# Reordering the first 285 entries of a hand-listed schedule in a fused Mamba-2 and SiLU-MLP kernel

## The chip, the cores and the metric

The kernel runs on one core of a Trainium2 chip. A core has five engines that run side by side and meet only through semaphores: TensorE (PE in the profile; its weight loads are shown as PEld), VectorE (DVE), ScalarE (ACT), GpSimd (POOL) and SyncE (SP), which here only issues DMAs. The metric is the device time of one launch in microseconds (us), a median over several runs.

## The reference, cut to what matters

The first half is a chunked state-space scan over 4 batches, 8 heads, 768 steps, head size 32 and state size 16. The second half sends its output, as 3,072 rows of 256, through an MLP.

```python
for c in range(nc):                       # chunks of the sequence
    cum = np.cumsum(log_a[chunk])
    M = (C @ B.T) * exp(cum_i - cum_j) * causal
    y = M @ x + (C @ state) * exp(cum)
    state = exp(sum(log_a)) * state + (B * exp(cum_end - cum)).T @ x
h = y @ w_in                              # 256 -> 2048
out = (h * sigmoid(h)) @ w_out            # 2048 -> 256
```

The two weight matrices come as 64-bit floats. The kernel loads them as pairs of 32-bit words and puts each 32-bit weight together from bits of both words.

## The kernel before, in words

The sequence is cut into 12 units of 256 steps, three to a batch, and two units form a pair. For each unit the scan part makes a decay mask, the product of C and B under that mask, the chunk states and the output y. The MLP then runs pair by pair. `w_in` and `w_out` are cut into 8 blocks each; the blocks of `w_in` are numbered 0 to 7, those of `w_out` 8 to 15.

Nothing is placed automatically. One string, `SCHEDULE`, lists 1,309 entries, and the last loop of the function walks it and calls a function for each. An entry is a name and its numbers: `w,4,2` calls `w_bits(4, 2)`. An entry sends its instructions to one fixed engine, or to the queue that issues its DMA, so the list sets the order in which each engine works; an engine never passes an instruction that waits. Across engines only data and buffers count. The entries that matter here, with their lines in the profile:

- `z` (L441): one 128x512 bf16 matmul on zeros, which does no work for the result and fills TensorE before there is work.
- `ia`, `ir`, `ip` (L375, L383, L379): loads of the decays `a` on SP. `A`, `AT`, `AU` (L448, L453, L457) clip them, transpose them on TensorE, and copy them out.
- `as`, `ab`, `E` (L495 on DVE or L497 on ACT, L502, L512): spread the decays, transpose them, and scan them on DVE to unit u's mask. `P01` (L475, L479): the prefix products, on DVE, from what `ip` loaded.
- `Ln`, `Lt`, `Lx` (L254, L262, L269): loads of B and C in two layouts and of x. An `Ln` moves 64 KB in 1,024 pieces, an `Lx` 128 KB in 1,024 pieces, an `Lt` 32 KB. The last number is the issuing queue: 0 is SP, 1 is ACT.
- `T` (L525), `tp`, `tq` (L531, L540), `ce` (L546): put C and B the other way round and scale them. `g0` (L585) multiplies them on TensorE into the banks `ga` and `gb`; `M` (L600) multiplies the result by the mask, on DVE.
- `B` (L520, POOL), `D` (L571), `S` (L613, L615, DVE), `SM` (L623, ACT): decayed B, its product with x, the running states, and the scaled states. `Y` (L635 with the states, L644 with the mask products) writes the unit's output over `ga` and `gb`; `X0` (L666, ACT) copies it out.
- `lw` (L288): the load of one weight block, 512 KB, on SP. `u`, `v` (L294, L297, ACT) turn its high and low words into floats. `w,n,0` and `w,n,1` (L303, L307, DVE) clip and shift the first; `w,n,2` (L310, DVE) puts the sign of the high word into the second. `W` (L318, POOL) adds both to the finished block. `H`, `lD`, `dD` (L322, L326, L330) split a block into parts.
- `s`, `si` (L697, L703): the first MLP product for one unit and one block, and SiLU. `n1` (L761): the second product of pair 0. `xh`, `x` (L679; L651 or L654): the split of y. `a`, `ax`, `d`, `dg` (L800, L811, L800, L821): the first product of later pairs in parts. `q` (L782): their second product.
- `AA`, `AD` (POOL), `AP` (DVE), `La`, `Lp` (SP): the decays of the later units, by way of DRAM.

`SLOTS` lists, for each of four buffer pools, which buffer each new tile takes, in the order of the list. A tile in a buffer that was used before waits until the last reader of the old tile is done.

Two lines show how an entry becomes an instruction and where the order comes from:

```python
            nc.vector.scalar_tensor_tensor(out=v, in0=hi, scalar=0x80000000, in1=v,
                                           op0=ALU.bitwise_and, op1=ALU.bitwise_or)
...
            f, *q = tok.split(",")
            DO[f](*map(int, q))
```

Of the kernel before, what the change touches and what calls it, by code (L numbers as in the profile page):

```python
# [15 lines left out]


SCHEDULE = """
Ln,0,0,0,1 ia,1 ci z,1 z,1 z,1 z,1 z,1 z,1 ia,0 Ln,0,0,1,1 cI z,1 ch cP ct ip,0,0 z,1 z,1 z,1 c1 cd A AT cp AU lw,0 z,1
z,1 as,0,0 ab,0,0 P01,0,0 P01,0,1 as,0,1 ab,0,1 as,1,1 ab,1,1 E,0,0 u,0 z,1 z,1 z,1 Lt,0,1,3,0 v,0 w,0,0 w,0,2 w,0,1  # L20
lw,4 W,0,1 z,1 B,0,0 z,1 z,1 v,4 Lt,0,1,1,0 u,4 z,1 z,1 Ln,1,1,1,0 z,1 E,0,1 B,0,1 z,1 z,1 z,1 Lt,0,1,0,0 Lt,0,1,2,0
T,0,1 as,1,0 z,1 z,1 z,1 tp,0 tq,0 E,1,1 Lx,0,0,0 Lx,0,1,0 D,0 S,0,0 z,1 w,4,2 z,1 S,0,1 z,1 w,4,0 S,0,2 ce,0,0 ce,0,1
g0,0 M,0,1 lw,7 v,7 Ln,1,0,0,0 SM,0,0 M,0,0 z,1 z,1 SM,0,1 u,7 w,4,1 w,7,0 z,1 z,1 w,7,2 w,7,1 lw,5 v,5 w,5,2 W,0,0
S,0,3 Ln,1,1,0,0 ab,1,0 E,1,0 C,0 Y,0 X0,0,1 Ln,1,0,1,0 B,1,1 X0,0,0 u,5 w,5,0 ip,1,0 z,1 P01,1,0 tp,1 tq,1 s,0,0 ce,1,1
ce,1,0 g0,1 Lx,1,1,0 Lx,1,0,0 W,4 xh,0 w,5,1 si,0,0 B,1,0 P01,1,1 D,1 s,0,4 M,1,1 lw,1 u,1 lw,12 S,1,0 W,5 v,1 ca S,1,1
S,1,2 SM,1,0 SM,1,1 lw,13 s,0,5 si,0,5 v,12 C,1 M,1,0 Y,1 w,1,0 w,1,1 W,7 si,0,4 lw,8 w,1,2 W,1,0 z,1 w,12,2 X0,1,0 H,7
S,1,3 X0,1,1 x,0,0 lD,7 u,12 w,12,0 w,12,1 u,13 w,13,0 w,13,1 W,1,1 s,0,1 u,8 v,8 s,1,5 ir,3 w,8,0 si,0,1 s,1,0 co
Ln,2,0,1,0 xh,1 W,12 x,1,0 w,8,1 v,13 w,13,2 W,13 lw,15 u,15 w,8,2 Ln,2,1,1,0 si,1,5 s,1,4 a,0,7 si,1,4 n1,9,0 H,12
Wd,12 x,0,1 lw,14 u,14 n1,11,0 n1,9,1 x,1,1 W,8 Ln,2,1,0,0 v,14 w,14,2 ir,0 si,1,0 n1,1,0 n1,1,1 H,0 n1,0,1 H,1 lw,6 v,6
w,6,2 n1,11,1 n1,10,1 ir,2 ir,1 u,6 lw,10 Wl,12 AA,0 AA,1 AD,4 w,6,0 AP w,6,1 AD,0 lw,2 Ln,2,0,0,0 ax,0,7 w,15,0 u,10  # L30
u,2 W,6 n1,8,0 AD,1 v,2 H,6 v,10 w,2,0 s,1,1 si,1,1 lw,3 tp,2 dD,7 v,3 v,15 u,3 w,2,1 w,2,2 W,2,0 Lt,3,1,3,0 lD,6 dD,6
w,14,0 n1,8,1 w,3,2 a,0,6 ax,0,6 w,15,2 W,2,1 s,1,2 si,1,2 H,2 d,0,7 w,14,1 dg,0,7 AD,2 w,3,0 w,15,1 d,0,6 dg,0,6 W,14
Lt,3,1,0,0 w,10,2 s,0,2 lw,9 u,9 v,9 Lt,3,1,2,0 Lt,3,1,1,0 T,3,1 H,4 si,0,2 n1,10,0 Lx,2,0,0 n1,12,1 La,2,0,0 w,3,1 tq,2
La,2,1,0 E,2,1 E,2,0 lD,4 w,9,0 W,15 n1,15,1 Lt,3,0,0,0 n1,12,0 B,2 ce,2,0 ce,2,1 Lt,3,0,3,0 g0,2 lw,11 u,11 Lp,2,0 C,2
M,2,1 Lx,2,1,0 gd,2 b,2,0 b,2,1 S,2,0 S,2,1 H,15 S,2,2 W,3 Lp,3,0 Lt,4,1,1,0 H,13 La,3,1,0 w,10,0 v,11 Lt,4,1,0,0
# [853 lines left out]
```

## Time and profile before

| what | value |
|---|---|
| three runs | 328.6, 329.49, 329.88 us; median 329.49 us |
| the profiled execution | 329.1 us, of which 327.4 us are the span of the instructions |
| granted TensorE clock, mean | 0.999 |
| busy share: PE, PEld, DVE, ACT, POOL | 98%, 74%, 73%, 64%, 17% |
| DMA | 29.27 MB in 94,962 packets |

The busy share is an average over stages. The first 18 us of the span hold loads, constants and unit 0's scan; the MLP's first useful matmul (L697) starts at 17.94 us. From there TensorE works without a break up to the last few microseconds. A row of the timeline gives the start, the length, the engine, the line and the tiles of some instructions in a row; in brackets stands how long the engine sat idle ahead of it and what ended that.

### The profile page before, as it was taken

To read this page: it belongs to the slowest core of one execution; us is meant where nothing else is said; L and a number is where in the kernel's file an instruction comes from. 1 tells how busy PE (TensorE), PEld (TensorE's weight loads), DVE (VectorE), ACT (ScalarE), POOL (GpSimd) and SP (SyncE) were. 2 spreads that over 40 slices of the span, in tenths; PEclk is the share of its full clock that TensorE was granted. 3 is DMA by queue.
4 is the path that set the end of the run, shared out by engine and by line. 5 is a ranking of instruction groups with operands and counts; after the bars stand their busy time and mean duration, and the time that the engine had idled before them with its cause. 6 is when DMAs were issued, how large, how long until landed. Compare 5 with 4: busy or idle time off the path is not lost.

```text
span 327.4 us, 7519 instructions
## 1 busy us (share of the span) xinstructions
PE 320.3 (98%) x3064; PEld 243.4 (74%) x3067; DVE 240.4 (73%) x331; ACT 209.5 (64%) x319; POOL 56.0 (17%) x74
## 2 busy tenths in 40 slices
...
GB/s 162 206 200 272 296 175 192 51 148 135 148 127 46 105 115 53 86 36 64 147 74 70 44 1 117 104 26 96 3 74 37 7 2 2 0 88 0 2 1 64
DMA packets 94962, 29.27 MB, mean 89 GB/s; under 512 B 80000, under 2 KB 86912, under 8 KB 94928
## 3 DMA queue, kind: packets, MB, share of 16 engines
...
## 4 chain that ended last, share of the span: by engine, by line
PE 94%; SPq 2%; DMA 1%; DVE 1%; issue 1%; DVEq 0%
PE hp L782 29%; PE ga L800 18%; PE gb L800 18%; PE hp L761 9%; PE hp L697 6%; PE o_ps L782 6%; PE ga L635 2%; PE ga L585 2%; PE ga L644 2%; DMA s2k<-in_C_dram 1%; PE gb L644 1%; PE ga L571 1%; SPq L262 0%; SPq L375 0%; PE o_ps L531 0%
## 5 line engine op out<-in xcount | busy, mean ns | idle before, releaser
L782 PE MATMUL hp<-r4k,s2k 128*128 128x512 f32 x400 | 110.0, 394 | 0.0
L651 DVE SCALAR_TENSOR_TENSOR r4k<-r4k,r4k 128x1024 fp32r<-128x1024 f32 (+1 forms) x42 | 50.5, 1202 | 51.3 <-ACT r4k L827 48.2
L782 PEld LDWEIGHTS hp<-r4k,s2k 128*128 128x128 f32 x400 | 74.0, 188 | 16.4 <-issue 0.3
L800 PE MATMUL ga<-raw,s2k 128*128 128x512 f32 x240 | 62.3, 395 | 0.0
L800 PE MATMUL gb<-raw,s2k 128*128 128x512 f32 x240 | 61.1, 390 | 0.0
L800 PEld LDWEIGHTS ga<-raw,s2k 128*128 128x128 f32 x240 | 44.7, 188 | 11.4 <-ACT ga L811 0.9
L800 PEld LDWEIGHTS gb<-raw,s2k 128*128 128x128 f32 x240 | 44.8, 188 | 9.9 <-ACT gb L811 0.5
L837 DVE SCALAR_TENSOR_TENSOR r4k<-r4k,r4k 128x1024 fp32r<-128x1024 f32 x40 | 49.2, 1231 | 3.4 <-DVE r4k L651 0.9
L827 ACT ACTIVATE r4k<-r4k 128x1024 fp32r<-128x1024 f32 x40 | 42.2, 1058 | 3.2 <-issue 1.3
L811 ACT ACTIVATE ga<-ga 128x1024 f32<-128x1024 f32 x21 | 21.1, 1007 | 24.6 <-PE ga L800 23.8
L811 ACT ACTIVATE gb<-gb 128x1024 f32<-128x1024 f32 x21 | 21.2, 1009 | 17.6 <-PE gb L800 13.3
L782 PE MATMUL o_ps<-r4k,s2k 128*128 128x512 f32 x80 | 30.7, 390 | 0.0
L761 PE MATMUL hp<-r4k,s2k 128*128 128x512 f32 x64 | 30.0, 602 | 0.0
L821 ACT ACTIVATE r4k<-gb 128x1024 f32<-128x1024 f32 x21 | 21.4, 1021 | 12.4 <-PE gb L800 9.9
L520 POOL TENSOR_TENSOR BT<-bn,ab 128x256 f32<-128x256 f32 x10 | 6.7, 672 | 129.5 <-DVE ab L512 123.3
L318 POOL TENSOR_TENSOR s2k<-s2k,s2k 128x512 uint32<-128x512 uint32 (+1 forms) x19 | 23.6, 1250 | 26.4 <-DVE s2k L307 13.7
L821 ACT ACTIVATE r4k<-ga 128x1024 f32<-128x1024 f32 x21 | 21.5, 1023 | 8.4 <-PE ga L800 8.2
L512 DVE TENSOR_TENSOR_SCAN ab<-ab,diag 128x512 f32<-128x512 f32 x20 | 24.8, 1265 | 0.0
L697 PE MATMUL hp<-r4k,s2k 128*128 128x256 f32 x96 | 22.3, 382 | 0.2 <-issue 0.2
L697 PEld LDWEIGHTS hp<-r4k,s2k 128*128 128x128 f32 x96 | 18.0, 190 | 4.0 <-issue 1.4
L761 PEld LDWEIGHTS hp<-r4k,s2k 128*128 128x128 f32 x64 | 11.6, 189 | 10.5 <-issue 9.6
L782 PEld LDWEIGHTS o_ps<-r4k,s2k 128*128 128x128 f32 x80 | 15.0, 188 | 3.2
...
## 6 DMA issues: line engine op xcount, KB each, us to landing
...
```

What stands on the lines that cost most here:

```text
L318: nc.gpsimd.tensor_tensor(out=u[:, :, fs], in0=u[:, :, fs], in1=v[:, :, fs], op=ALU.add)
L512: nc.vector.tensor_tensor_scan(out=o, data0=src, data1=diag.rearrange("p h t -> p (h t)"), initial=0.0, op0=ALU.mult, op1=ALU.add)
L644: nc.tensor.matmul(out=y[w][32 * q:32 * q + 32, c, 64 * k:64 * k + 64], lhsT=xc[64 * c:64 * c + 64, k, h], rhs=m[64 * c:64 * c + 64, k, h] ...
L651: nc.vector.scalar_tensor_tensor(out=l, in0=f32(h), scalar=BACK, in1=y, op0=ALU.mult, op1=ALU.add)
L697: nc.tensor.matmul(out=hp[:, i], lhsT=WT[j][:, kc, 128 * i:128 * i + 128], rhs=XM()[:, 2 * kc:2 * kc + 2, u], start=(kc == 0), stop=(kc == ...
L761: nc.tensor.matmul(out=NP[m], lhsT=WT[8 + f // 2][:, f % 2, 128 * m:128 * m + 128], rhs=GT[0, f // 2][:, f % 2], start=(n == 1), stop=(n = ...
L782: nc.tensor.matmul(out=ACC[P, c], lhsT=WK[8 + i, p][:, k, 128 * m:128 * m + 128], rhs={"h": HT, "l": LT, "d": DT}[p][P, i][:, k], start=(n ...
L800: nc.tensor.matmul(out=o, lhsT=WK[j, q][:, kc, 128 * i:128 * i + 128], rhs=xs[:, 2 * kc:2 * kc + 2], start=(start and q == "h" and kc == 0 ...
L811: nc.scalar.activation(t, t, AF.Copy, scale=1.0 + Z)
L821: nc.scalar.activation(g, t, AF.Silu, scale=BACK)
L827: nc.scalar.activation(t, GT[G, i], AF.Copy, scale=-LESS * Z)
L837: nc.vector.scalar_tensor_tensor(out=DT[G, i], in0=f32(HT[G, i]), scalar=-1.0, in1=f32(LT[G, i]), op0=ALU.mult, op1=ALU.subtract)
```

## The change

The first 285 entries of `SCHEDULE` stand in another order; the entries themselves are the same, and from there on the list is as it was. `SLOTS` is written anew to fit. From about entry 460 on every tile follows the same earlier tile in its buffer as before, only the buffer's number differs. In the order of each engine:

- DVE: `T,0,1` comes before `w,0,1`; `w,4,2`, which stood between `S,0,0` and `S,0,1`, now stands behind `M,0,0` and `M,0,1`. `E,1,0` comes before `w,7,0`, and `w,5,2` is now the last of block 5's three steps. `x,0,1` and `x,1,1` come later, `x,1,1` behind `w,15,2`.
- ACT: `tq,0` and `ce,0,1` come ahead of `u,4` and `v,4`, `ce,0,0` behind them. `SM,0,1` stands before `u,7`, `SM,0,0` between `u,7` and `v,7`.
- TensorE: fourteen `z` stand before `AT` where there were ten; one `z` that stood behind `Y,1` has moved ahead of `s,0,0`. Seven `z` now stand between `ab,0,0` and `tp,0`, with `ab,0,1` and `ab,1,1` behind `tp,0`. In the pair-0 part some `n1` and `s` change places.
- SP: `ir,3` is now second in the queue, and `ir,1`, `ir,0`, `ir,2` are earlier. `lw,4` moves from sixth to twelfth, behind the four `Lt,0` and behind both `Ln,1,1`. The order of later blocks is 12, 8, 13, 2, 6, 14, 10, 15, 3 where it was 12, 13, 8, 15, 14, 6, 10, 2, 3.
- POOL: `ca` and `co`, three memsets, come first; `W,4` comes before `B,1,1`; `W,1` before `W,7`; `AA,1` and `AA,0` come around `W,13`. The two `Ln` on ACT's queue change places.

```diff
-Ln,0,0,0,1 ia,1 ci z,1 z,1 z,1 z,1 z,1 z,1 ia,0 Ln,0,0,1,1 cI z,1 ch cP ct ip,0,0 z,1 z,1 z,1 c1 cd A AT cp AU lw,0 z,1
-z,1 as,0,0 ab,0,0 P01,0,0 P01,0,1 as,0,1 ab,0,1 as,1,1 ab,1,1 E,0,0 u,0 z,1 z,1 z,1 Lt,0,1,3,0 v,0 w,0,0 w,0,2 w,0,1
-lw,4 W,0,1 z,1 B,0,0 z,1 z,1 v,4 Lt,0,1,1,0 u,4 z,1 z,1 Ln,1,1,1,0 z,1 E,0,1 B,0,1 z,1 z,1 z,1 Lt,0,1,0,0 Lt,0,1,2,0
-T,0,1 as,1,0 z,1 z,1 z,1 tp,0 tq,0 E,1,1 Lx,0,0,0 Lx,0,1,0 D,0 S,0,0 z,1 w,4,2 z,1 S,0,1 z,1 w,4,0 S,0,2 ce,0,0 ce,0,1
-g0,0 M,0,1 lw,7 v,7 Ln,1,0,0,0 SM,0,0 M,0,0 z,1 z,1 SM,0,1 u,7 w,4,1 w,7,0 z,1 z,1 w,7,2 w,7,1 lw,5 v,5 w,5,2 W,0,0
-S,0,3 Ln,1,1,0,0 ab,1,0 E,1,0 C,0 Y,0 X0,0,1 Ln,1,0,1,0 B,1,1 X0,0,0 u,5 w,5,0 ip,1,0 z,1 P01,1,0 tp,1 tq,1 s,0,0 ce,1,1
-ce,1,0 g0,1 Lx,1,1,0 Lx,1,0,0 W,4 xh,0 w,5,1 si,0,0 B,1,0 P01,1,1 D,1 s,0,4 M,1,1 lw,1 u,1 lw,12 S,1,0 W,5 v,1 ca S,1,1
...
+ca Ln,0,0,1,1 ia,0 Ln,0,0,0,1 co ch ir,3 ia,1 ci ct z,1 z,1 z,1 z,1 c1 z,1 z,1 z,1 cP ip,0,0 z,1 cp Lt,0,1,3,0 z,1 z,1
+lw,0 z,1 Ln,1,1,1,0 cd A cI Lt,0,1,2,0 z,1 z,1 Lt,0,1,0,0 Lt,0,1,1,0 z,1 AT AU as,0,1 as,0,0 as,1,1 P01,0,0 P01,0,1 z,1
+Ln,1,1,0,0 ab,0,0 E,0,0 z,1 z,1 u,0 z,1 z,1 w,0,0 z,1 z,1 T,0,1 z,1 as,1,0 w,0,1 B,0,0 tp,0 tq,0 ab,0,1 E,0,1 B,0,1 lw,4
+v,0 ce,0,1 w,0,2 Lx,0,1,0 ab,1,1 C,0 E,1,1 W,0,1 z,1 z,1 z,1 Lx,0,0,0 u,4 z,1 z,1 lw,7 v,4 z,1 z,1 ce,0,0 D,0 S,0,0
+S,0,1 Ln,1,0,0,0 z,1 g0,0 w,4,0 z,1 z,1 S,0,2 SM,0,1 M,0,0 u,7 W,0,0 M,0,1 z,1 SM,0,0 z,1 z,1 w,4,2 w,4,1 lw,5 v,7 w,7,2
+ab,1,0 W,4 Y,0 X0,0,0 z,1 X0,0,1 E,1,0 w,7,0 Ln,1,0,1,0 tp,1 ip,1,0 P01,1,0 u,5 w,5,0 tq,1 ce,1,1 ce,1,0 Lx,1,0,0 S,0,3
+ir,1 w,5,1 v,5 P01,1,1 Lx,1,1,0 w,7,1 lw,1 s,0,0 si,0,0 ir,0 g0,1 w,5,2 u,1 B,1,1 B,1,0 M,1,1 D,1 S,1,0 S,1,1 v,1 s,0,4
+C,1 S,1,2 SM,1,0 SM,1,1 W,5 si,0,4 s,0,5 si,0,5 M,1,0 w,1,0 lw,12 w,1,2 w,1,1 W,1,0 W,1,1 Ln,2,0,1,0 u,12 v,12 Y,1
...
+u,14 lw,15 AP AD,1 n1,11,1 Ln,2,0,0,0 n1,9,0 s,1,1 n1,10,1 si,1,1 u,10 lw,3 Wd,12 u,3 x,0,1 AD,0 Ln,2,1,1,0 w,14,2
+n1,8,0 n1,0,1 v,10 H,0 tp,2 dD,7 v,3 v,15 w,2,0 w,2,1 w,2,2 W,2,0 Lt,3,1,3,0 Wl,12 u,15 lD,6 dD,6 w,14,0 n1,8,1 w,3,2
+a,0,6 H,1 ax,0,6 w,15,2 W,2,1 s,1,2 si,1,2 H,2 x,1,1 d,0,7 w,14,1 dg,0,7 AD,2 w,3,0 w,15,0 w,15,1 d,0,6 dg,0,6 W,14
...
     "raw": """
-0 1 2 3 4 5 6 0 1 2 3 4 5 6 0 2 5 6 3 4 0 1 5 6 2 4 0 3 5 6 1""",
+0 1 2 3 4 5 6 0 1 2 3 4 5 6 0 2 1 6 3 4 0 5 1 6 2 4 0 3 1 6 5""",
```

More of the change, by code (lines that the diff above doesn't have):

```diff
@@ L24 @@
-S,0,3 Ln,1,1,0,0 ab,1,0 E,1,0 C,0 Y,0 X0,0,1 Ln,1,0,1,0 B,1,1 X0,0,0 u,5 w,5,0 ip,1,0 z,1 P01,1,0 tp,1 tq,1 s,0,0 ce,1,1
-ce,1,0 g0,1 Lx,1,1,0 Lx,1,0,0 W,4 xh,0 w,5,1 si,0,0 B,1,0 P01,1,1 D,1 s,0,4 M,1,1 lw,1 u,1 lw,12 S,1,0 W,5 v,1 ca S,1,1
-S,1,2 SM,1,0 SM,1,1 lw,13 s,0,5 si,0,5 v,12 C,1 M,1,0 Y,1 w,1,0 w,1,1 W,7 si,0,4 lw,8 w,1,2 W,1,0 z,1 w,12,2 X0,1,0 H,7
-S,1,3 X0,1,1 x,0,0 lD,7 u,12 w,12,0 w,12,1 u,13 w,13,0 w,13,1 W,1,1 s,0,1 u,8 v,8 s,1,5 ir,3 w,8,0 si,0,1 s,1,0 co
-Ln,2,0,1,0 xh,1 W,12 x,1,0 w,8,1 v,13 w,13,2 W,13 lw,15 u,15 w,8,2 Ln,2,1,1,0 si,1,5 s,1,4 a,0,7 si,1,4 n1,9,0 H,12
```

17 lines of the change are left out of this document (8 added, 9 removed), and 6 rows, old and new, of the table SLOTS.

## The prediction

> **What bounds the kernel now.** I read the page's engine and chain lines first, then the busy time by stretches, then TensorE's waits after 18 us. In the stretches the first pair of columns is the length and PE's busy time; the DMA share and GB/s come last.
>
> ```profile
> PE 320.3 (98%) x3064; PEld 243.4 (74%) x3067; DVE 240.4 (73%) x331; ACT 209.5 (64%) x319; POOL 56.0 (17%) x74
> ...
> PE 94%; SPq 2%; DMA 1%; DVE 1%; issue 1%; DVEq 0%
> ```
>
> ```profile
> 6.00:12.00 6.00, 5.70 (x47) 3.33 (x46) 5.72 (x11) 4.01 (x8) 1.93 (x4) 1.00 0.93 186
> 12.00:18.00 6.00, 5.27 (x166) 3.37 (x153) 5.78 (x13) 4.23 (x12) 1.25 (x3) 1.00 0.93 219
> ...
> 30.00:50.00 20.00, 20.00 (x76) 13.58 (x75) 19.15 (x26) 16.26 (x28) 12.99 (x14) 1.00 0.81 232
> ...
> 90.00:320.00 230.00, 230.00 (x2005) 185.43 (x2004) 156.19 (x184) 144.64 (x193) 15.69 (x20) 1.00 0.30 54
> ```
>
> ```profile
> PE hp L697 <- issue: 0.2, 1, 0.2
> ```
>
> TensorE is busy for all of the 230 us from 90 to 320, and its only wait between 18 and 320 us is the 0.2 us of the last line. So behind the first `s` matmul the end is that matmul's start plus a fixed amount of TensorE work. An order that issues the same work can gain only ahead of that start; it loses wherever a block comes later than TensorE asks for it. DVE, at 19.15 of 20 us between 30 and 50, is the engine with least room.
>
> What sets the start? TensorE's timeline:
>
> ```profile
> 1.27 4.45 PE L441 MATMUL o_ps<-s2k 128*128 128x512 bf16 x10 [1.27 <-DVE s2k L388]
> 5.65 0.31 PE L453 MATMUL o_ps<-ident,s2k 32*128 32x32 f32 x1
> 6.24 0.59 PE L441 MATMUL o_ps<-s2k 128*128 128x512 bf16 x2 [0.28 <-DVE s2k L457]
> ...
> 8.07 3.40 PE L441 MATMUL o_ps<-s2k 128*128 128x512 bf16 x15
> ...
> 13.63 0.28 PE L585 MATMUL gb<-ce,bh 32*64 32x128 f32 x2
> ...
> 15.73 0.27 PE L635 MATMUL ga<-cw,sm 32*64 32x64 f32 x2 [0.42 <-DVE ab L600]
> ...
> 17.94 1.99 PE L697 MATMUL hp<-r4k,s2k 128*128 128x256 f32 x8
> ...
> 21.07 3.77 PE L697 MATMUL hp<-r4k,s2k 128*128 128x256 f32 x16
> ```
>
> `s,0,0` starts at 17.94. Two things arrive there together: unit 0's output (mask products on DVE, `Y,0` from 15.73, `X0` on ACT), and `tp,1`, which stands in front of `s,0,0` and waits for the DMA `Ln,1,0,1`:
>
> ```profile
> 17.54 0.31 PEld L531 LDWEIGHTS o_ps<-ident,s2k 128*128 128x128 f32 x3 [0.36 <-DMA s2k<-in_B_dram]
> ```
>
> **The change, part by part.** *1. `w,4,2` behind the masks.* DVE's rows:
>
> ```profile
> 7.50 1.20 DVE L512 TENSOR_TENSOR_SCAN ab<-hp,diag 128x512 f32<-128x512 f32 x1
> ...
> 11.30 0.65 DVE L525 STREAM_TRANSPOSE ct<-s2k 128x256 f32<-128x256 f32 x1 [0.21 <-DMA s2k<-in_C_dram]
> ...
> 12.98 0.68 DVE L310 SCALAR_TENSOR_TENSOR s2k<-raw,s2k 128x512 uint32<-128x512 uint32 x1
> 13.58 0.28 DVE L615 SCALAR_TENSOR_TENSOR st<-st,s2k,hp 128x64 f32<-128x64 f32 x1
> ...
> 14.30 0.69 DVE L600 TENSOR_TENSOR ab<-gb,ab 128x512 f32<-128x512 f32 x1
> 14.90 0.69 DVE L600 TENSOR_TENSOR ab<-ga,ab 128x512 f32<-128x512 f32 x1
> 15.50 0.42 DVE L307 TENSOR_SCALAR s2k<-s2k 128x512 uint32<-128x512 uint32 x1
> ```
>
> It holds DVE from 12.98 to 13.58: 0.60 us off the way to the masks. `T` waited 0.21 for the last `Lt`; with `lw,4` no longer ahead of the `Lt` loads I take that wait as gone too. Gain on DVE: 0.81.
>
> *2. Four more `z` ahead of `AT`.* `AT` waits for them in order. The ten before it took 0.43 each (first row of TensorE's timeline), the fifteen from 8.07 on 0.22, and the two at 6.24 were fast already (0.59 for both). The four cost 4 x 0.22 = 0.86 or 4 x 0.43 = 1.71; the rate changed between 5.5 and 6.3 us, so I take one slow and three fast: 1.08. `AU`, `as`, `P01` and the first mask scan (7.50) all follow `AT`, with DVE busy from there on, so the masks would start at 14.30 + 1.08 - 0.81 = 14.57. The first part's gain is spent here. The Trainium skill ("TensorE: Matmul & The Clock Gate", Part 1, What's actually happening) says that the clock opens after a free-running window of about 3.4 us, so that the switch falls at a different point in each run. The trace agrees with a switch (0.43, then 0.22), but shows one execution; by that rule all four could be slow, which rival D prices from the rows.
>
> *3. SP's queue.* The same loads stand ahead of `Ln,1,0,1`, plus `ir,3`.
>
> ```profile
> 2.50 0.63 SPq L379 DMA_DIRECT2D s2k<-in_a_dram  x1
> 3.17 0.46 SPq L288 DMA_DIRECT2D raw<-in_moe_w_in_dram  x1
> ...
> 6.84 2.98 SPq L269 DMA_DIRECT2D s2k<-in_x_dram  x2
> ```
>
> Issues go by place in the queue: `ip`, the first big load, moves from third (2.50) to fourth (3.17), so the stream starts 0.67 later. From 6 to 18 us the DMA share is 0.93, so little of that is made up: I take 0.67 for everything up to `Ln,1,0,1`, bounds 0 (the idle 7% of 12 us is 0.84) and 1.3 (`lw,0` itself moves two places). `lw,4` and `lw,7` now also have `Ln,1,1,0` ahead of them. ACT's rows show when blocks 4, 7 and 5 landed:
>
> ```profile
> 10.29 0.69 ACT L297 ACTIVATE s2k<-raw 128x512 f32<-128x512 uint32 x1 [1.77 <-DMA raw<-in_moe_w_in_dram]
> 10.87 0.67 ACT L294 ACTIVATE s2k<-raw 128x512 f32<-128x512 f32 x1
> ...
> 12.21 0.91 ACT L546 ACTIVATE ce<-ct,par 128x256 f32<-128x256 f32 x2
> 14.32 0.68 ACT L297 ACTIVATE s2k<-raw 128x512 f32<-128x512 uint32 x1 [1.21 <-DMA raw<-in_moe_w_in_dram]
> 14.91 0.62 ACT L623 ACTIVATE sm<-st,par 128x96 f32<-128x96 f32 x2
> ...
> 16.66 0.68 ACT L297 ACTIVATE s2k<-raw 128x512 f32<-128x512 uint32 x1 [0.56 <-DMA raw<-in_moe_w_in_dram]
> ```
>
> An `Ln` behind a block costs 17.54 - 16.66 = 0.88. Block 7 lands at 14.32 + 0.67 + 0.88, about 15.85; block 4 at 10.29 + 0.67 + 0.88 and some 0.4 for `Lt` loads that it shared the stream with, about 12.2 (bounds 11.0 without a new load ahead, 13.0 with both `Ln,1,1` in full).
>
> *4. ACT.* `u,4` and `v,4` (0.58 each, 10.29 to 10.87) now stand between `ce,0,1` and `ce,0,0`, which waits for block 4: 12.2 + 1.16 + 0.50 = 13.9; `g0` ended 0.8 after `ce` before (13.91 against 13.12), so the masks start at 14.7, 0.13 behind DVE's own 14.57, and end at 14.7 + 1.29 = 16.0 (before 15.59). Then `u,7` stands between the two halves of `SM`: 15.85 + 0.58 + 0.30 = 16.75. Before, `v,7` stood ahead of both and they were done at 15.53, just ahead of the masks; so the scaled states, and not the masks, now end last. `Y,0` starts at 16.8 and `s,0,0`, 2.21 later as before, at 19.0: 1.07 late. `tp,1`, at 17.54 + 0.67, is done by 18.7 and costs nothing; without this cover it would cost 0.7.
>
> *5. Block 5.* `s,0,5` started at 22.9 (21.07 plus half of 3.77).
>
> ```profile
> 19.81 0.50 DVE L475 TENSOR_SCALAR s2k<-s2k 128x256 f32<-128x256 f32 x1
> 20.23 0.42 DVE L307 TENSOR_SCALAR s2k<-s2k 128x512 uint32<-128x512 uint32 x1
> 20.57 0.69 DVE L479 TENSOR_TENSOR_SCAN s2k<-s2k,s2k 128x260 f32<-128x260 f32 x1
> ```
>
> ```profile
> 20.73 1.59 POOL L318 TENSOR_TENSOR s2k<-s2k,s2k 128x512 uint32<-128x512 uint32 x1 [0.57 <-DVE s2k L307]
> ```
>
> Before, block 5 left DVE at 20.65, 5.06 after the masks, and POOL's add ended at 22.3, 0.6 early. Now `w,4,2` (0.60) and `P01,1,1` (0.69) have also come ahead of its last step: 5.06 + 0.60 + 0.69 - 0.2 of old idle time is 6.15. I add 0.2 for `v,7`, due at 17.3, and 0.4 for `P01,1,0`, whose load `ip,1` comes 0.67 later (needed at 19.4; no row shows its landing: 0 if it came by 18.7 before, 1.1 if just at 19.81). 16.0 + 6.75 + 1.59 = 24.3, against 22.9 + 1.07 = 24.0 for TensorE: the stall is 0.3, and TensorE is 1.4 late at `s,0,5`. The `z` behind `Y,1` is gone: -0.2.
>
> *6. Later.* Behind `s,0,1` I find no new wait. `W,1`, `W,12`, `W,8`, `W,13` are finished 1 us or more before their matmuls. POOL's three memsets and `cI` lie ahead of `AT`'s new time. Tightest is `x,1,1`, now behind `w,3,2` and `w,15,2`, since `d,0,7` needs it:
>
> ```profile
> L654 DVE SCALAR_TENSOR_TENSOR r4k<-r4k,r4k 128x512 fp32r<-128x512 f32 x2 | 3.5, 1772 | 0.0
> ```
>
> ```profile
> 42.88 1.89 PE L697 MATMUL hp<-r4k,s2k 128*128 128x256 f32 x8
> ...
> 49.29 1.27 PE L800 MATMUL gb<-r4k,s2k 128*128 128x512 f32 x4
> ...
> 53.04 3.60 PE L761 MATMUL hp<-r4k,s2k 128*128 128x512 f32 x8
> ```
>
> From the end of `s,1,1` ACT has seven steps of the kinds above, 0.5 to 0.6 each (`si,1,1` to `v,3`, some 3.9), then DVE 0.6 + 0.6 + 1.77: about 6.95. TensorE took 4.6 from there to `d,0,7` (44.7 to 49.29) and now has three more `n1` in between, two of the L761 matmuls at 0.43 each, so 7.2. Room 0.25, so 0; bounds 0 and 0.8. The earlier `AA` and `AD` bring unit 2's masks no later. New buffers bring no later last reader.
>
> Sum: 1.07 + 0.3 - 0.2 = **+1.2 us**. Against the profiled 329.1 us (its 327.4 us span and 1.7 around it) that is 330.3; that execution lies 0.4 under the median of the three runs, and on the median 329.49 it is 330.7.
>
> **Rivals.** *A. The stream catches up.* If the DMA's idle 7% swallows the 0.67, and `Ln,1,1,0` fills a hole too, blocks 4 and 7 land about as before; the masks start at 14.57, 0.27 late, less 0.2 for the `z`: 329.5. For it: all these loads pass anyway. Against: 0.93 is almost full. At best, without the `z` cost, the masks start when `g0` allows, about 13.95: 0.35 and 0.2 gained, 328.9, and `tp,1`, with `Ln,1,0,1` at 17.54, forbids more. That is no measurable gain either; a faster kernel needs that load to land 1.5 us sooner.
>
> *B. Slower past the bound: block 7 very late.* Two issues of 1,024-piece loads in a row held SP for 2.98 (last SP row). If such a hold falls right ahead of `lw,7` while nothing else is queued, block 7 lands some 1.5 us after my 15.85, at 17.3; `SM` ends at 18.2, `s,0,0` starts at 20.45, 2.5 late, 2.3 without the `z`: 331.8. It decides from block 7 at 16.7 on. For it: the holds are there. Against: the stream had work queued during them.
>
> *C. `d,0,7` or `s,0,5` waits longer.* Up to 0.8 at `x,1,1` plus 0.5 at block 5 beside my sum: 332.0. For it: DVE's 19.15 of 20 us. Against: its work up to `d,0,7` is the same.
>
> *D. All four `z` slow*, at 0.43: `AT` 0.63 later, masks from 15.2 (not 14.7), so block 5 ends 0.5 later: 331.2.
>
> **How the numbers follow.** Half a per cent, 1.65 us, is about what a measurement of this kernel can tell from no change: 327.85 to 331.1. My forecast (330.7, own range 330.0 to 331.1) has 0.42; A 0.16, of which 0.02 on the faster side; B 0.20; C 0.11 and D 0.06, all but 0.01 of the two above 331.1. What I have not seen has 0.05: 0.03 faster, 0.02 slower. So faster 0.05, within 0.57, slower 0.38. The range, 328.9 to 332.7, leaves out about 0.1 on each side.
>
> **What would show it.** Right: `AT` near 6.7; `T` without a wait; DVE's L310 for block 4 behind the two L600; L623 split around an L294; `s,0,0` near 19; a wait of L697 on POOL L318 near 24; from 50 us on the old timeline, 1.2 later. Wrong: `s,0,0` before 18.2 (A), block 7 after 16.7 (B), or TensorE waits past 30 us (C).

## The result and the profile after

| | before | after |
|---|---|---|
| median | 329.08 us (4 runs) | 331.36 us (331.26 to 331.79, 4 runs) |
| ratio, 95% interval | | 1.0067, 1.0047 to 1.0087 |
| the profiled execution, its span | 329.1, 327.4 us | 331.79, 330.1 us |
| last TensorE product ends (read from the trace) | 323.59 | 326.27 |

The change costs 2.3 us, where 1.2 were forecast. The median is slower by a little more than the half per cent that I took as the bound, though the interval reaches down to just below it. It lies 0.3 above the likeliest case's own range (330.0 to 331.1) and inside the wide one. The profiled execution lost 2.7 us.

The engine line and the chain line of the page of the kernel after; TensorE's busy time is the same to 0.3 us, so no work was added where it counts, only waits:

```profile
PE 320.6 (97%) x3067; PEld 243.0 (74%) x3067; DVE 241.3 (73%) x331; ACT 209.1 (63%) x319; POOL 58.2 (18%) x74
...
PE 85%; DMA 4%; DVE 3%; SPq 2%; POOL 2%; ACT 2%; issue 1%; DVEq 0%
```

TensorE's timeline after (start, us, engine, line, operation, what it waited for), to be held against the rows of before in the prediction:

```profile
1.27 4.96 PE L441 MATMUL o_ps<-s2k 128*128 128x512 bf16 x14 [1.27 <-DVE s2k L388]
6.15 0.24 PE L453 MATMUL o_ps<-ident,s2k 32*128 32x32 f32 x1
...
13.73 0.53 PE L571 MATMUL hp<-s2k,BT 64*32 64x64 f32 x32 [1.22 <-DMA s2k<-in_x_dram]
...
20.03 0.55 PE L531 MATMUL o_ps<-ident,s2k 128*128 128x128 f32 x3 [1.14 <-DMA s2k<-in_B_dram]
20.41 1.89 PE L697 MATMUL hp<-r4k,s2k 128*128 128x256 f32 x8
...
28.34 7.17 PE L697 MATMUL hp<-r4k,s2k 128*128 128x256 f32 x32
...
49.81 1.89 PE L697 MATMUL hp<-r4k,s2k 128*128 128x256 f32 x8
52.03 1.19 PE L800 MATMUL gb<-r4k,s2k 128*128 128x512 f32 x4 [0.34 <-DVE r4k L654]
53.20 1.20 PE L800 MATMUL ga<-r4k,s2k 128*128 128x512 f32 x4
54.24 1.89 PE L697 MATMUL hp<-r4k,s2k 128*128 128x256 f32 x8
```

Two stretches of the kernel before that are compared with these, the row of `s,0,1` and the two around `d,0,7` and `d,0,6`:

```profile
26.41 7.07 PE L697 MATMUL hp<-r4k,s2k 128*128 128x256 f32 x32 [0.16 <-issue]
...
47.75 1.89 PE L697 MATMUL hp<-r4k,s2k 128*128 128x256 f32 x8
...
51.31 1.89 PE L697 MATMUL hp<-r4k,s2k 128*128 128x256 f32 x8
```

`s,0,0` starts at 20.41 instead of 17.94, right behind a `tp,1` that waited for its load. Then part comes back: `s,0,1` starts at 28.34 instead of 26.41, 1.93 late. And at `d,0,7` more is lost: from `s,1,2` to `s,0,2`, with `d,0,7` and `d,0,6` between them, it took 54.24 - 49.81 = 4.43 us where the kernel before took 3.57 (47.75 to 51.31, with unrounded times). So there are two places, 1.9 and 0.86 us; another 0.1 was lost between them, and 0.2 came back later.

DVE's rows after:

```profile
7.94 1.20 DVE L512 TENSOR_TENSOR_SCAN ab<-hp,diag 128x512 f32<-128x512 f32 x1
10.04 0.43 DVE L303 TENSOR_SCALAR s2k<-s2k 128x512 f32<-128x512 f32 x1 [0.90 <-ACT s2k L294]
10.38 0.65 DVE L525 STREAM_TRANSPOSE ct<-s2k 128x256 f32<-128x256 f32 x1
...
14.29 0.23 DVE L613 COPY st<-hp 128x64 f32<-128x64 f32 x1 [0.17 <-PE hp L571]
...
15.67 0.68 DVE L600 TENSOR_TENSOR ab<-ga,ab 128x512 f32<-128x512 f32 x1
16.27 0.68 DVE L600 TENSOR_TENSOR ab<-gb,ab 128x512 f32<-128x512 f32 x1
16.87 0.68 DVE L310 SCALAR_TENSOR_TENSOR s2k<-raw,s2k 128x512 uint32<-128x512 uint32 x1
```

The change did what it says: `w,4,2` is behind the two masks. But the masks start at 15.67 instead of 14.30. DVE stood for 0.90 us ahead of `w,0,0` and for 0.17 ahead of `S,0,0`. ACT's rows say why, and show the collision at 41 us beside GpSimd's:

```profile
9.32 0.69 ACT L294 ACTIVATE s2k<-raw 128x512 f32<-128x512 f32 x1 [1.51 <-DMA raw<-in_moe_w_in_dram]
...
12.18 0.67 ACT L294 ACTIVATE s2k<-raw 128x512 f32<-128x512 f32 x1 [0.41 <-DMA raw<-in_moe_w_in_dram]
...
15.79 0.38 ACT L623 ACTIVATE sm<-st,par 128x96 f32<-128x96 f32 x1 [1.98 <-DVE st L615]
16.07 0.67 ACT L294 ACTIVATE s2k<-raw 128x512 f32<-128x512 f32 x1
16.64 0.36 ACT L623 ACTIVATE sm<-st,par 128x96 f32<-128x96 f32 x1
...
45.09 0.63 ACT L322 ACTIVATE s2k<-s2k 128x512 fp32r<-128x512 f32 x1 [4.17 <-POOL s2k L318]
```

```profile
41.36 3.69 POOL L318 TENSOR_TENSOR s2k<-s2k,s2k 128x512 uint32<-128x512 uint32 x1
```

Block 0 reached ACT at 9.32; in the trace its load landed at 9.29, against 6.83 before. And `W,6` took 3.69 us, where the same row of the kernel before reads:

```profile
41.70 1.28 POOL L318 TENSOR_TENSOR s2k<-s2k,s2k 128x512 uint32<-128x512 uint32 x1
```

### The profile page after: what moved, and what is told of

Same layout as the page of the kernel before. It is cut to its first block, busy times and chain, and to the rows that moved or that the text cites. A ratio compares the mean times of both kernels' runs of the same rounds, so it can differ in the third digit from the quotient of the medians.

```text
span 330.1 us, 7522 instructions
## 1 busy us (share of the span) xinstructions
PE 320.6 (97%) x3067; PEld 243.0 (74%) x3067; DVE 241.3 (73%) x331; ACT 209.1 (63%) x319; POOL 58.2 (18%) x74
## 4 chain that ended last, share of the span: by engine, by line
PE 85%; DMA 4%; DVE 3%; SPq 2%; POOL 2%; ACT 2%; issue 1%; DVEq 0%
PE hp L782 28%; PE ga L800 17%; PE gb L800 17%; PE hp L761 6%; PE o_ps L782 6%; PE hp L697 3%; DMA s2k<-in_B_dram 2%; PE ga L585 2%; DMA raw<-in_moe_w_in_dram 2%; POOL s2k L318 2%; PE ga L635 1%; PE ga L644 1%; DVE s2k L310 1%; PE ga L571 1%; PE gb L644 1%
## 5 line engine op out<-in xcount | busy, mean ns | idle before, releaser
L651 DVE SCALAR_TENSOR_TENSOR r4k<-r4k,r4k 128x1024 fp32r<-128x1024 f32 (+1 forms) x42 | 51.5, 1228 | 51.0 <-ACT r4k L827 50.3
L318 POOL TENSOR_TENSOR s2k<-s2k,s2k 128x512 uint32<-128x512 uint32 (+1 forms) x19 | 25.4, 1344 | 24.8 <-DVE s2k L310 13.2
```

Source lines behind the costliest of these rows:

```text
L318: nc.gpsimd.tensor_tensor(out=u[:, :, fs], in0=u[:, :, fs], in1=v[:, :, fs], op=ALU.add)
L651: nc.vector.scalar_tensor_tensor(out=l, in0=f32(h), scalar=BACK, in1=y, op0=ALU.mult, op1=ALU.add)
```

## The experiments

The kernels built from the kernel before have their line numbers one higher (L601 is its L600). The table is read from the traces: the start of unit 0's first mask, of `s,0,0` and of `s,0,1`, how long `W,6` took, the time from `s,1,2` to `s,0,2`, which stands behind `d,0,7` and `d,0,6`, and the end of the last TensorE product against 323.59. The ratio is that of the timed runs to the kernel before on the same chip.

| kernel | mask | s,0,0 | s,0,1 | W,6 | s,1,2 to s,0,2 | end | ratio (95%) |
|---|---|---|---|---|---|---|---|
| before | 14.30 | 17.94 | 26.41 | 1.28 | 3.57 | 0 | 1 |
| after | 15.67 | 20.41 | 28.34 | 3.69 | 4.43 | +2.7 | 1.0067 (1.0047 to 1.0087) |
| e1 | 15.43 | 18.82 | 27.88 | 3.69 | 4.41 | +2.2 | 1.0053 (1.0028 to 1.0078) |
| e2 | 16.00 | 19.29 | 28.45 | 3.69 | 4.42 | +3.1 | 1.0042 (1.0015 to 1.0069) |
| e3 | 14.06 | 19.35 | 27.48 | 1.28 | 3.57 | +1.0 | 0.9995 (0.9969 to 1.0021) |
| e4 | 15.50 | 18.89 | 27.94 | 4.29 | 5.04 | +3.1 | 1.0081 (1.0061 to 1.0100) |
| e5 | 16.22 | 19.59 | 28.66 | 3.69 | 4.44 | +3.3 | 1.0079 (1.0051 to 1.0108) |
| e6 | 15.47 | 19.05 | 29.64 | 1.28 | 3.56 | +2.9 | 1.0050 (1.0028 to 1.0073) |
| e7 | 15.40 | 19.94 | 28.13 | 4.31 | 4.43 | +2.5 | 1.0057 (1.0039 to 1.0074) |
| e8 | 13.91 | 18.41 | 26.60 | 1.28 | 3.57 | 0.0 | 1.0001 (0.9978 to 1.0024) |
| r1 | 15.46 | 18.86 | 27.91 | 1.29 | 3.57 | +1.5 | 1.0034 (1.0015 to 1.0053) |
| r3 | 15.51 | 18.89 | 27.95 | 3.68 | 4.48 | +2.3 | 1.0056 (1.0037 to 1.0076) |
| r4 | 15.74 | 20.71 | 28.91 | 3.69 | 4.45 | +3.3 | 1.0077 (1.0047 to 1.0108) |
| r5 | 16.22 | 21.74 | 29.84 | 1.37 | 3.56 | +3.6 | 1.0048 (1.0033 to 1.0064) |

One step of 0.86 us is 0.26% and about as wide as half an interval, so each single step rests on its trace, and the ratios only bear it out. A trace is one execution: `s,0,0` and the end of e2, e7, r4 and r5 hold a stretch at half the TensorE clock that the others don't have (see r4 and r5).

### e1: the load of `tp,1` ahead of a weight block

```diff
- lw,7 ... Ln,1,0,0,0 ... lw,5 ... w,7,0 Ln,1,0,1,0 tp,1
+ lw,7 ... Ln,1,0,0,0 ... Ln,1,0,1,0 lw,5 ... w,7,0 tp,1
```

> Changed kernel with the second block's B load `Ln,1,0,1` issued ahead of `lw,5` on SP's queue, nothing else moved. Three theories for `s,0,0` at 20.41. Theory fetch: the load's last 14 packets stood behind the 16,384-byte read of TensorE's own instructions (17.69 to 18.93 us, one DMA engine). Theory order: the load lands near 20.0 because `lw,5` is ahead of it in the stream. Theory masks: the chain masks, SM, Y, X0 on DVE and ACT sets `s,0,0`. Fetch and order both expect the load to be complete by 18.5, `tp,1`'s second transpose by 18.7 and `s,0,0` at 19.1, where X0 (18.65 + about 0.4) sets it: 1.3 us sooner, 330.1 us against 331.4. Masks expects `s,0,0` to stay at 20.4 and no change of the time.

`tp,1` no longer waited and `s,0,0` started at 18.82, as expected. The time hardly moved. TensorE's and DVE's rows of e1 show where the gain went:

```profile
18.82 1.89 PE L697 MATMUL hp<-r4k,s2k 128*128 128x256 f32 x8
21.92 1.99 PE L697 MATMUL hp<-r4k,s2k 128*128 128x256 f32 x8
24.57 1.96 PE L697 MATMUL hp<-r4k,s2k 128*128 128x256 f32 x8 [0.66 <-DVE st L615]
```

```profile
23.82 0.42 DVE L551 TENSOR_TENSOR cw<-o_ps,s2k 128x256 f32<-128x256 f32 x1
24.15 0.27 DVE L615 SCALAR_TENSOR_TENSOR st<-st,s2k,hp 128x64 f32<-128x64 f32 x1
```

`s,0,5` takes the PSUM buffer that `D,1` wrote, and the last to read that is `S,1,2`, which left DVE at 24.42. In the kernel before `S,1,2` left at 21.76 + 0.97 = 22.73 (three L615 in one row, given below) and TensorE was just free. So the wait has the name that the view gives it, and it is not `W,5`, which I had named in step 5: that ended at 24.08 here. Of the 1.59 that e1 gained at `s,0,0`, 0.46 is left at `s,0,1`: no more than that is what the late load cost the profiled execution.

```profile
21.76 0.97 DVE L615 SCALAR_TENSOR_TENSOR st<-st,s2k,hp 128x64 f32<-128x64 f32 x3
22.64 0.42 DVE L551 TENSOR_TENSOR cw<-o_ps,s2k 128x256 f32<-128x256 f32 x1
```

The 1.69 of `S,1,2` in e1 are 1.13 at the masks, 0.34 between the first mask of unit 0 and that of unit 1 (6.88 before, 7.22 here, with `w,4,2` now inside), and the rest from `C,1` (L551), which the change put ahead of `S,1,2`.

### e2 and e3: moving the read of TensorE's instructions

In the profiled execution after, the last 14 packets of `Ln,1,0,1` started at 18.92, when all others had started by 17.68. One DMA engine was busy from 17.69 to 18.93 with a packet of 16,384 bytes from another queue, the one that the page calls "q8 instruction": 24 packets in the whole run, about one for every 256 of TensorE's matmuls and weight loads together. So I take them for reads of TensorE's instructions; nothing in the trace names the engine. The Trainium skill ("DMA: Bandwidth & Descriptors", Queues, rings and completion order) says that a DMA engine takes whole packets from its queues in turn. The packets of that execution agree; the next two kernels were to show it.

```diff
  (e2, from after: ten z entries go)
- u,0 z,1 z,1 w,0,0 z,1 z,1 T,0,1 z,1 as,1,0
+ u,0 z,1 w,0,0 z,1 T,0,1 as,1,0
- W,0,1 z,1 z,1 z,1 Lx,0,0,0 u,4 z,1 z,1 lw,7 v,4 z,1 z,1 ce,0,0
+ W,0,1 z,1 Lx,0,0,0 u,4 z,1 lw,7 v,4 z,1 ce,0,0
- w,4,0 z,1 z,1 S,0,2
+ w,4,0 z,1 S,0,2
- M,0,1 z,1 SM,0,0 z,1 z,1 w,4,2
+ M,0,1 z,1 SM,0,0 w,4,2
  (e3, from before: three small fillers, 64 columns each)
- ab,1,0
+ z,0,3 ab,1,0
```

> Changed kernel without ten of the 21 `z` between `AT` and `Y,0` (20 TensorE instructions fewer ahead of `Y,0`, the fourteen ahead of `AT` kept, SP's queue as it was). Theory fetch: the read of instructions comes some 20 instructions later in `Y,0`, 0.2 us later, at about 17.9, when the load's packets are through; the load completes by 18.6, `s,0,0` starts at 19.1 and the time falls by 1.3 us to 330.1, as in the run before this. Theory order: SP's queue is the same, so the load still lands near 20.0 and `s,0,0` stays at 20.4, 331.4 us; if the missing `z` cost clock, slower. Theory masks: no change.

> Kernel before, with three 64-column filler products (six TensorE instructions) ahead of `ab,1,0`, nothing else. Theory fetch: the read of instructions, which started at 16.64 in `Y,0`, comes six instructions sooner, at 15.5 to 16.1, in front of the packets of `Ln,1,0,1`; the load, complete at 17.5 in the kernel before, is held to 18.3 or later, `tp,1`'s second transpose goes from 17.54 to 18.4 or later and `s,0,0` from 17.94 to 18.7 or later: 0.8 us or more slower, 329.9 or more against 329.1. Theories order and masks: nothing of theirs is touched, the load stays at 17.5, 329.1 us.

In e2 the read came at 18.44, and the load was complete at 18.33; `s,0,0` started at 19.29. In e3 the read came at 15.42, the load was complete at 18.93 instead of 17.50, and `tp,1` waited:

```profile
18.97 0.55 PE L532 MATMUL o_ps<-ident,s2k 128*128 128x128 f32 x3 [1.68 <-DMA s2k<-in_B_dram]
```

That is the expected size, but not the expected mechanism: the read was over at 16.66 and the load's last packet started at 17.41, and still one of its sixteen landings came 1.5 us later. In other kernels with the load order of the changed kernel (e4, e7, r1, r3) the read began anywhere between 16.28 and 17.01, and the load was complete between 18.07 and 18.38. In e8 it was late again by 0.5, with the read over at 16.67. So a late last landing of this load is shown in three of the profiled executions; that the read causes it is shown by packets once only, and stays open. It is not what makes the change slower: e1, e2, e4, r1 and r3 have no wait at `tp,1` and are slower all the same, and e3's timed runs are level with the kernel before.

### e4: `x,1,1` sooner

```diff
- x,0,1 AD,0 ... H,2 x,1,1 d,0,7
+ x,0,1 x,1,1 AD,0 ... H,2 d,0,7
```

> Changed kernel with `x,1,1` (VectorE, line 654) right behind `x,0,1` instead of just ahead of `d,0,7`. The wait of 0.34 us of `d,0,7` for it goes. If that wait alone costs what the spacing of TensorE's instructions shows between 49.3 and 52.0, the gap between the two kernels falls by 0.3 to 0.6: 330.8 to 331.1 against 331.4. If VectorE's work just ahead of it (the weights' sums, fed late by ScalarE and GpSimd) sets it, the next wait takes its place and the time stays 331.4.

The rival was right, and more: the wait went from `x,1,1` to the next in line and grew. `W,6`, with one more DVE operation in front, took 4.29, all of ACT came later, and `d,0,6`, right behind `d,0,7`, waited for a bank that `ax,0,6` on ACT still held. TensorE's row:

```profile
53.41 1.20 PE L800 MATMUL ga<-r4k,s2k 128*128 128x512 f32 x4 [1.20 <-ACT ga L811]
```

### e5 and e6: the order of loads against the order of work

```diff
  (SP's loads up to ip,1: before, and e5)
  ia,1 ia,0 ip,0 lw,0 Lt,0,1,3 lw,4 Lt,0,1,1 Ln,1,1,1 Lt,0,1,0 Lt,0,1,2 Lx,0,0 Lx,0,1 lw,7 Ln,1,0,0 lw,5 Ln,1,1,0 Ln,1,0,1
  (after, and e6)
  ia,0 ir,3 ia,1 ip,0 Lt,0,1,3 lw,0 Ln,1,1,1 Lt,0,1,2 Lt,0,1,0 Lt,0,1,1 Ln,1,1,0 lw,4 Lx,0,1 Lx,0,0 lw,7 Ln,1,0,0 lw,5 Ln,1,0,1
```

> Changed kernel with SP's queue put back: its loads up to `ip,1` (and `ir,3`) go out in the order of the kernel before, every other entry stays. The loss at `s,0,1` (26.41 before, 28.34 in the changed kernel, 27.9 where `tp,1` was in time) has two theories left. Theory queue: `lw,0` two places later makes VectorE wait 0.90 us for `u,0` at 9.14, and the x loads behind `lw,4` make it wait for `D,0`; VectorE has no gap from there to `Y,1`, so the masks (14.30 to 15.67) and `s,0,1` come 1.4 to 1.5 later. It expects masks near 14.5, `s,0,1` at 26.4 to 26.9 and a ratio to the kernel before of 1.0025 to 1.0035 (what is left is lost at `d,0,7`). Theory fillers: the four `z` more ahead of `AT` and the order of the computing entries set it; masks stay at 15.3 or later, `s,0,1` at 27.9 or later, ratio 1.0055 to 1.0067.

> Kernel before with only SP's queue of the changed kernel up to `ip,1` (`ir,3` among it), every other entry as before. Theory queue: `u,0` and `D,0` come as late as in the changed kernel, masks at 15.3 or later, `s,0,1` 1.0 to 1.5 later than 26.41, ratio 1.003 to 1.0045. Theory fillers: `AT` stays at 5.65, masks near 14.3 to 14.6, ratio 0.999 to 1.001.

e6 took the step that theory queue expects. Its load of block 0 landed at 8.87 (6.83 in the kernel before), and DVE's rows show the same 0.90 as the changed kernel, and masks 1.17 late:

```profile
9.59 0.43 DVE L304 TENSOR_SCALAR s2k<-s2k 128x512 f32<-128x512 f32 x1 [0.90 <-ACT s2k L295]
...
15.47 0.69 DVE L601 TENSOR_TENSOR ab<-gb,ab 128x512 f32<-128x512 f32 x1
```

`Y,1` came 1.25 late (26.02 against 24.77). What is more in its `s,0,1` (29.64) is a wait of 1.77 inside `Y,1` that the profile puts down to "issue": no engine and no load held TensorE. A read of instructions started at 26.22, and only at 28.77 did TensorE go on:

```profile
28.77 0.29 PE L645 MATMUL gb<-ab,s2k 64*32 64x64 f32 x8 [1.77 <-issue]
```

That wait is seen in this one execution (332.04 us). e6's twelve timed runs spread from 329.95 to 332.75 us, so how often it comes is not known.

But e5 fell out against theory queue: with the loads back in their old order the new order of work is no better, masks at 16.22, 1.0079. Its block 0 came at 7.24 and did not hold DVE; `T`, which the change had moved ahead of two scans, now waited 1.14 us for the last `Lt`, which landed at 10.75 behind `lw,4`. So neither half is the cause alone. Each order of work asks for the loads in its own order; the old pair fits, the new pair and both mixed pairs don't.

### e7 and r1: the collision at `W,6`

```diff
  (e7)
- AD,4 v,6 H,12 ... w,6,2 W,6 H,6
+ v,6 H,12 ... w,6,2 W,6 AD,4 H,6
  (r1)
- w,6,2 W,6 H,6 ... AP ... x,0,1 ... v,15 w,2,0 w,2,1
+ w,6,2 w,2,0 W,6 H,6 ... AP ... x,0,1 ... v,15 w,2,1
```

> Changed kernel with `AD,4` (GpSimd's issue of the transfer of `az`) right behind `W,6` instead of ahead of it, nothing else moved. Theory collision: in the changed kernel `W,6` started at 41.36, in the middle of VectorE's scan and of four more operations without a gap, and took 3.69 us (1.28 in the kernel before); ScalarE's `H,6` waited 4.17 us for it and passed the delay on to `v,3`, `v,15`, `w,14,2`, `x,1,1` and `d,0,7`, which cost 0.86 us. With `W,6` at 40.75, straight behind `w,6,2`, it takes 1.3 to 1.7 us, `d,0,7` follows its neighbour without a wait, and the ratio falls from 1.0067 to 1.004. Rival: `d,0,7` is late because VectorE has more work ahead of it, whatever `W,6` does: the wait and 1.0067 stay.

> Changed kernel with `w,2,0` (VectorE, line 303) moved up to right behind `w,6,2`, so that this is what VectorE runs when GpSimd's `W,6` arrives, and no longer the scan of line 486 with four more operations behind it. Theory collision: where `W` met an operation of lines 303, 307, 310 or 651 it got in behind that one, and took 1.3 to 1.7 us while VectorE's next operation was held; so `W,6` should end near 42.2 instead of 45.05, `H,6` on ScalarE start there, `d,0,7` follow without its wait of 0.34, and the 0.86 us lost between 49.3 and 54.2 come back: ratio 1.004 instead of 1.0067. Rival, VectorE simply has too much to do ahead of `x,1,1`: `W,6` may be short, but `d,0,7` waits as before, 1.0067.

In e7 `W,6` started sooner and took 4.31, to 44.85: GpSimd's transfer in front had nothing to do with it. The change moved `AP`, the scan of line 486, from ahead of `w,6,1` to behind `w,6,2`, so `W,6`, which waits for `w,6,2`, now arrives in the middle of that scan. What it ran beside, in the changed kernel, are these DVE rows:

```profile
40.58 1.23 DVE L486 TENSOR_TENSOR_SCAN r4k<-r4k,r4k 48x520 f32<-48x520 f32 x1
41.73 0.66 DVE L654 SCALAR_TENSOR_TENSOR r4k<-r4k,r4k 128x512 fp32r<-128x512 f32 x1
42.31 0.68 DVE L310 SCALAR_TENSOR_TENSOR s2k<-raw,s2k 128x512 uint32<-128x512 uint32 x1
42.91 0.68 DVE L330 SCALAR_TENSOR_TENSOR s2k<-s2k,s2k 128x512 fp32r<-128x512 f32 x1
43.52 0.41 DVE L303 TENSOR_SCALAR s2k<-s2k 128x512 f32<-128x512 f32 x1
43.96 1.38 DVE L307 TENSOR_SCALAR s2k<-s2k 128x512 uint32<-128x512 uint32 x1
```

Five DVE operations run without a gap at their usual length, the sixth takes 1.38 instead of 0.42, and `W,6` ends at 45.05 inside it. That reads as `W,6` working only from 43.8 on, its usual 1.28, with DVE standing by. In r1 `w,2,0` stands first, and waits 0.29 for its input; GpSimd gets in, and DVE is the one that stands:

```profile
40.51 2.01 DVE L303 TENSOR_SCALAR s2k<-s2k 128x512 f32<-128x512 f32 x1 [0.29 <-ACT s2k L294]
42.44 1.23 DVE L486 TENSOR_TENSOR_SCAN r4k<-r4k,r4k 48x520 f32<-48x520 f32 x1
```

```profile
50.89 1.27 PE L800 MATMUL gb<-r4k,s2k 128*128 128x512 f32 x4
52.00 1.08 PE L800 MATMUL ga<-r4k,s2k 128*128 128x512 f32 x4
52.92 1.89 PE L697 MATMUL hp<-r4k,s2k 128*128 128x256 f32 x8
```

`W,6` took 1.29, `d,0,7` had no wait, the stretch is 3.57 again, and the end of TensorE's work is as late as `s,0,1` and no later (1.5). The table has no exception: wherever `W,6` took 3.68 or more, 0.84 us or more were lost at `d,0,7`, and nowhere else. The ratio fell from 1.0067 to 1.0034.

### e8: the namesake alone

```diff
- S,0,0 z,1 w,4,2 ... M,0,1 ... M,0,0 z,1
+ S,0,0 z,1 ... M,0,1 ... M,0,0 w,4,2 z,1
```

> Kernel before with `w,4,2` moved behind the two masks of unit 0, nothing else. By step 1 of the prediction the masks start 0.60 sooner, at 13.7, and `Y,0` by as much if ScalarE's `ce` allows it; `s,0,0` still stands behind `tp,1` at 17.54, and VectorE's work ahead of `Y,1` is the same, so the time is that of the kernel before: ratio 0.9995 to 1.0005, at the most 0.2 us better. A rival that the move by itself pays expects 0.3 to 0.6 us, 0.998 to 0.999.

DVE's row of the first mask:

```profile
13.91 0.68 DVE L601 TENSOR_TENSOR ab<-gb,ab 128x512 f32<-128x512 f32 x1
```

The masks gained 0.39 of the 0.60 and `Y,0` as much (15.34); `s,0,0` did not, behind `tp,1`. The time is that of the kernel before.

### r3: ten `z` ahead of `AT`

```diff
- lw,0 z,1 Ln,1,1,1,0 cd A cI Lt,0,1,2,0 z,1 z,1 Lt,0,1,0,0 Lt,0,1,1,0 z,1 AT
+ lw,0 Ln,1,1,1,0 cd A cI Lt,0,1,2,0 Lt,0,1,0,0 Lt,0,1,1,0 AT
```

> Changed kernel without the four `z` nearest ahead of `AT` (ten are left, as in the kernel before). Step 2 of the prediction charged them 1.08 us on the way to the masks: by it the masks start 0.4 to 1.1 sooner than 15.67 and the time falls by as much, ratio 1.0035 to 1.0055. The rival from the trace: VectorE waited 0.90 us for `u,0` at 9.14, behind `AU`, `as`, `P01` and the first scan, because block 0 landed at 9.29; whatever `AT` gains is waited out there: masks within 0.2 of 15.4 to 15.7, ratio 1.0055 to 1.0067.

The rival of the expectation was right. `AT` was at 5.65 and the first scan at 7.50, as in the kernel before, and then DVE waited for block 0 and for the `Lt` loads. DVE's rows:

```profile
9.10 0.43 DVE L303 TENSOR_SCALAR s2k<-s2k 128x512 f32<-128x512 f32 x1 [0.39 <-ACT s2k L294]
10.22 0.65 DVE L525 STREAM_TRANSPOSE ct<-s2k 128x256 f32<-128x256 f32 x1 [0.70 <-DMA s2k<-in_C_dram]
...
15.51 0.68 DVE L600 TENSOR_TENSOR ab<-ga,ab 128x512 f32<-128x512 f32 x1
```

### r4 and r5: loads sooner, and the repairs together

```diff
  (r4; r5 too, with Ln,1,0,1 ahead of lw,5, ten z as in r3, and w,2,0 as in r1)
- ia,0 ir,3 ia,1 ip,0 Lt,0,1,3 lw,0 ... Lt,0,1,1 Ln,1,1,0 lw,4 Lx,0,1 Lx,0,0 lw,7
+ ia,0 ia,1 ip,0 lw,0 Lt,0,1,3 ... Lt,0,1,1 Lx,0,1 Lx,0,0 Ln,1,1,0 lw,4 lw,7 ... ip,1 ir,3
```

> Changed kernel with three moves in SP's queue: `lw,0` ahead of `Lt,0,1,3`, the two `Lx,0` ahead of `Ln,1,1,0` and `lw,4`, `ir,3` behind `ip,1`; all computing entries as they were. Theory queue (loads of unit 0 and block 0 set VectorE's chain): block 0 lands near 8.0 instead of 9.29, `D,0`'s x near 12.6 instead of 13.60, the `Lt` loads a little later (10.2), so `T` may wait 0.2; the masks start at 14.9 to 15.3 instead of 15.67 and `s,0,1` follows them 12.4 to 12.9 later, as in the runs so far: 27.3 to 28.1, ratio 1.0045 to 1.006. If the computing order alone set it, masks stay at 15.4 to 15.7.

> The repairs together: the loads as in the run before this and also `Ln,1,0,1` ahead of `lw,5`, ten `z` ahead of `AT`, and `w,2,0` right behind `w,6,2`. If the three causes add up, masks near 14.7, `s,0,1` near 27.2, no wait of `d,0,7`: ratio 1.0015 to 1.003. It beats the kernel before only if `Y,1` too comes sooner than 24.77, which needs VectorE's masks at 14.3 or sooner; I don't expect that.

Both expectations for the masks failed. In r4 block 0 was in time (landed at 7.18) and so was x (`D,0` at 12.05), but block 4 then landed at 13.21, and `ce,0,0` stands behind it on ACT. ACT's row, and DVE's:

```profile
13.24 0.66 ACT L294 ACTIVATE s2k<-raw 128x512 f32<-128x512 f32 x1 [2.11 <-DMA raw<-in_moe_w_in_dram]
```

```profile
15.74 0.69 DVE L600 TENSOR_TENSOR ab<-ga,ab 128x512 f32<-128x512 f32 x1 [0.77 <-PE gb L585]
```

In r5 the same wait was 1.66 and the masks came at 16.22. Block 0, x and block 4 are needed by three engines within a few us of each other; whichever load goes back sets the masks. r5's repair at `W,6` held (1.37, 3.56). Neither is shown to beat the changed kernel with r1's move alone, and no kernel here beats the kernel before.

Part of what these two lose ahead of `s,0,0` is not due to their order alone. In r4 the scaled states were done at 16.19 and the masks at 17.03, but `Y,0` started only at 18.63. The clock that the profile gives as granted to TensorE was 0.50 from 15.54 on for 3.4 us; the five `z` behind `g0` took 2.31 us (1.25 would be usual) and the four L502 products 1.06 (usually 0.60). In r5 the clock was 0.50 for 6.8 us from 14.24 on. That execution, at 332.74 us, is the slowest of r5's twelve, whose median is 331.09, so the table's +3.6 overstates r5 and the ratio is the better figure. The same came over e2 from 13.18 on and e7 from 14.89 on, for 3.4 us each: e7's first mask is as early as r1's (15.40 and 15.46), its `s,0,0` is 1.08 later. In e2 and r5 it fell late in a wait of TensorE (1.9 and 2.6 us), in e7 and r4 1.6 and 0.6 us behind one (1.5 and 1.7 us); but in r3 and e6 TensorE waited 1.7 us there too and the clock stayed at 1.00, so what sets it off is open. The changed kernel, e1 and r1 stayed at 1.00 throughout this stretch.

## Why the prediction was right or wrong

*The number.* 330.7 forecast, 331.36 measured, on the wrong side of the half per cent. The loss at `s,0,1` was forecast at 1.07 + 0.3 - 0.2 = 1.2 and is 1.5 where `tp,1` is in time (e1, e4, r1, r3), 1.7 and 2.0 in e7 and e2, where the clock fell to 0.50 on the way, and 1.9 in the profiled execution. That 1.2 and 1.5 lie so close is in part luck: the masks came 0.97 later than forecast, and most of that hid behind the scaled states, which I had ending 0.75 after the masks (steps 3 and 4). The step that failed in size is step 6: 0 forecast, 0.86 measured, just outside its own bounds of 0 and 0.8.

*Step 1, `w,4,2`.* Right that it brings nothing at the end (e8). The 0.60 are 0.39 at the masks. `T`'s wait went, as forecast.

*Step 2, the `z`.* Wrong as a term. `AT` came at 6.15, not 6.7, since the rate of the `z` changed sooner in this execution; and what it lost is covered by DVE's waits for block 0 and for the `Lt` loads (0.39 and 0.70 in r3). The clock's switch does fall differently in each execution: `AT` behind the same fourteen `z` came at 6.05 to 6.94 in eight kernels.

*Step 3, SP's queue.* This step had the cause in hand and missed it. Block 4 (12.18 against 12.2) was right and block 7 near (the load landed at 15.34, against 15.85), but I did not follow block 0. It moved two places back, behind `ir,3` and the first `Lt`; it was issued 0.98 later and landed 2.46 later, where my widest bound was 1.3. Where the other 1.5 went in the stream is not shown. In the profiled execution block 0 held DVE for 0.90, and the masks start at 15.67 where I had 14.7, and end at 16.95 where I had 16.0. Block 0 alone does not set them, though: with this order of loads it landed anywhere from 8.36 (r3) to 9.29, and the masks came at 15.40 to 15.67 all the same, for DVE then waited for `Lt` instead (r3); with block 0 in time (r4) it was block 4, and the masks came at 15.74.

*Step 4, ACT.* `SM` in two halves around `u,7`, `Y,0` at 17.10 (16.8 forecast), and `s,0,0` at 18.8 to 18.9 in e1, e4, r1 and r3 (19.0 forecast): right in place and size. The path was in part another: block 7 had landed 0.45 before `SM,0,1` started, and what `SM,0,1` had waited for, 1.98 us, was `S,0,2` on DVE, which ended just ahead of the late masks. So the scaled states (17.00) and the masks (16.95) end together, near the 16.75 that I had for the states alone. The sentence that failed is that `tp,1` "is done by 18.7 and costs nothing"; in the profiled execution it was done at 20.4. It cost 0.46 at the end, not the 1.4 by which `s,0,0` missed my 19.0, for TensorE would have waited at `s,0,5` anyway.

*Step 5, block 5.* The place was right, the cause was not. `W,5` ended at 24.08 (e1) and 24.47 (after), 24.3 forecast. But what `s,0,5` waited for was its PSUM buffer, read last by `S,1,2` on DVE, with `C,1` newly in front of it. The wait was 0.66 in e1, against 0.3.

*Step 6, later.* I counted the steps to `x,1,1` and gave each its usual duration. I looked at the blocks on GpSimd that TensorE wants at once, and not at `W,6`, whose reader is `H,6` on ACT, in front of everything that feeds DVE there. With `W,6` at 3.69 instead of 1.28 the sum of steps was 2.4 short. The terms add up to 6.87 rather than 6.95, a room of 0.3, which changes nothing. In r1, with `W,6` short, no wait is left, so there was room; how much, no run shows.

*Rivals.* C came true in its place (`d,0,7`), but by `W,6` and not by DVE's own load; A and B did not happen. D's condition, slow `z`, matters only up to the waits for block 0 and `Lt`.
